# Linear attention and a tanh-shrink MLP on one core: reading the state one product ahead of the output, issuing eight half loads from GpSimd, and making the last unit's inner factors after another product

## The chip, the core and the metric

The kernel runs on one core of a Trainium2 chip. The core has a matrix engine (PE, with its weight loads shown as PEld), a vector engine (DVE), an activation engine (ACT), GpSimd (POOL) and a queue engine (SP). Each takes its instructions in the order of its own queue and waits on semaphores for what the others have made. Transfers are issued here from SP and POOL, a few from ACT at the very start, and all are carried by the same 16 DMA engines.

The metric is the device time of one execution in microseconds (us). The kernel before takes 670.73 us, the median of three runs between 670.1 and 672.22. An execution that was profiled gives the times inside.

## The reference

Chunks of decayed linear attention run along the sequence with one state per batch and head; then each token goes through a two-layer network with `h - tanh(h)` between the layers.

```python
# q, k, v: (B=4, H=8, S=768, D=64); lam: one decay per head
for b in range(nb):                                   # blocks of 64 positions
    intra = einsum('bhic,bhjc->bhij', qb, kb) * Dmask[None]
    intra = einsum('bhij,bhjd->bhid', intra, vb)
    inter = einsum('bhid,bhde->bhie', qb * lam_pow[None], kv_state)
    out[:, :, sl] = intra + inter
    kv_state = lam_block * kv_state + einsum('bhsd,bhse->bhde', kb * rev_pow, vb)

x = out.transpose(0, 2, 1, 3).reshape(3072, 512)
h = x @ w_in                                          # 512 x 2048
result = (h - tanh(h)) @ w_out                        # 2048 x 512
```

The two weight matrices come as 64-bit floats; the kernel makes 32-bit floats of them itself.

## The kernel before

**Tiling.** The kernel takes 128 positions of all four batches at a time, so there are six groups g of 512 tokens. Within a group a chunk (g, b) is one batch's 128 positions. The attention of a group is done for two pairs of batches, (0, 1) and (2, 3). The hidden layer's 2048 columns are four units u of 512. Block products are done by Strassen-like schemes with seven products (P1 to P7) in place of eight: from group 1 on for the output layer (`down`, `down_twice`), where most of the seven are themselves made of seven smaller ones, and for groups 2 to 5 for the input layer too (`inner_steps`).

**Attention of a chunk pair.** `att_transpose` turns q and k round (on PE for groups 0 and 1, on DVE later) and makes `qd`, the decayed q. `att_scores` makes the masked scores `ss`. `att_out` then issues, on PE: products that read the old state into two PSUM banks `ops` (line 420, 32 small ones in a pair); on ACT, four decays of the state in place (line 423), which may only begin when those reads are done; on PE, products with the scores (line 429), the new key-value products (line 394), and more score products (line 439), which carry an explicit dependency on the first of the four decays; on DVE the sum of state and key-value products (line 449); on ACT the two evacuations to `xt` (line 451).

**The first 104 us.** Group 0's input layer is done plainly by `up_plain(u, cs)` (line 798): for one unit and one quarter c of its output, 16 matmul records of 256 columns in the trace, then a tanh on ACT (line 805) and a subtraction on DVE (line 806). While these products run, the raw weights are loaded, rounded on ACT (lines 309 to 311, three operations a block) and DVE (lines 313 and 314, two operations a block), and four staging tiles `raw64` go round: a load waits until ACT has read the block four before it. Blocks of `w_in` are loaded from SP (lines 226 and 229), blocks of `w_out` from POOL (line 224). A list `turns` says which quarter product comes next, how many blocks to round after it, and which piece of group 1's attention to run: `p0` for batches 0 and 1, `p1` for 2 and 3. `p0[2:]`, the decays of k and `att_out(1, (0, 1))`, stands behind the product (3, 21).

**Loads of q, k and v.** `load_natural` brings a chunk in one transfer for q and three each for k and v: heads 0 to 3 in one, and heads 4 to 7 in two, with the two halves of 64 rows exchanged. For group 0 the exchanged halves come from ACT (batch 0) or POOL; from group 1 on all come from SP. Chunks (1, 0) and (1, 1) are asked for by `load(B + 2)`, on line 891, ahead of the `turns`; the blocks of `w_in` that are not yet asked for stand behind them in SP's queue.

**Group 1 on.** The hidden layer of a group runs over units u. At the end of each unit of group 1, `inner_weights(u)` makes the inner factors of that unit's `w_in`, which group 2 on will use: for each of three factors, four small additions on DVE (line 572) into a tile of the ring `sums` (six tiles, shared with the sums that `sums_twice` and `inner_tokens` make) and one store of 192 KB from POOL to DRAM (line 573). Group 1's output products follow in this order: P2, `att_out(2, (0, 1))`, P4, the transposes of batches 2 and 3, P5, their scores, the decays of k (line 385), P6, `att_out(2, (2, 3))`, P7, then P3 together with group 2's inner products. Within `down_twice` the seven small products come in the order 1, 2, 6, 5, 7, 3, 4; the sixth needs a sum that DVE makes while the product runs (line 748). The factors of the small products come from DRAM through a ring of seven tiles `wb`, issued by POOL (lines 648, 651 and 654), each load waiting until PE has left the tile seven before it.

**What sets the order.** The framework's planner lays out each engine's queue, taking operations that it holds for ready, the earlier in the program first. Operations wrapped in `tied` or `keep_in_program_order` keep the order of the program among each other: all loads of q, k and v, the DVE transposes (line 349), the additions of `inner_weights` and the decays of k of group 2 are of this kind. Everything else may be drawn ahead.

Of the kernel before, what the change touches and what calls it, by code (L numbers as in the profile page):

```python
# [9 lines left out]
F32 = mybir.dt.float32  # L10
# [14 lines left out]
def kernel(  # L25
# [32 lines left out]
    nc = tc.nc  # L58
# [75 lines left out]
    chunks = [(g, b) for g in range(NG) for b in range(B)]  # L134
    at = {"loaded": 0}

    def load_natural(g, b, names):
        for name, src, bufs in (("q", q, 2), ("k", k, 3), ("v", v, 4)):
            if name in names:
                x = (qpool if name == "q" else io).tile([128, H, D], F32, name=f"{name}_nat", tag=name, bufs=bufs)  # L140
                rows = src[b, :, ts(g, BLK), :].rearrange("h s d -> s h d")
                if name == "q":
                    parts = [(nc.sync, x, rows)]
                else:
                    eng = nc.sync if g > 0 else nc.scalar if b == 0 else nc.gpsimd
                    parts = [(nc.sync, x[:, 0:4], rows[:, 0:4])] + [
                        (eng, x[ts(1 - t, HALF), 4:8], rows[ts(t, HALF), 4:8]) for t in range(2)]
                for eng, to, of in parts:
                    tc.keep_in_program_order(eng.dma_start(out=to, in_=of))
                raw[g, b][name] = x  # L150

    hold = {}

    def load_blocks(g, half):

        for name, src in (("q", q), ("k", k)):
            x = late["blk"].tile([128, 2 * NP, BLK // 32, 32], F32, name=f"{name}_blk", tag="blk")
            heads = src[ts(half, 2)].rearrange("b (p j) s d -> j s (b p) d", j=2)
            for r in range(BLK // 32):
                for c in range(4):  # L160
                    op = tc.keep_in_program_order(nc.sync.dma_start(
                        out=x[ts(c, 32), :, r], in_=heads[c // 2, g * BLK + 32 * r:g * BLK + 32 * (r + 1), :, ts(c % 2, 32)]))
                    if g in hold:

                        tc.add_manual_dep(op.ins, hold.pop(g).ins.name, mybir.DependencyInfo(
                            mybir.DependencyClass.Sync, mybir.DependencyReason.DATA), reason="begin")
            for n in range(2):
                raw[g, 2 * half + n][name + "b"] = x[:, ts(n, NP)]

# [230 lines left out]
        kv = kv_products(g, bs)  # L400
        tied(True, nc.scalar.activation(state[:, bs[0]:bs[0] + 2], kv, AF.Copy))

    def att_out(g, bs):
        half = bs[0] // 2
        xt[g, half] = xpool.tile([128, KI, HB], F32, name=f"xt{half}", tag=f"xt{half}")
        st = state[:, bs[0]:bs[0] + 2]

        ops = [bank("op", "att", 4).rearrange("d (p b s) -> d p b s", p=2, b=2) for _ in range(2)]

        def dst(n, p, j):  # L410
            return ops[p // 2][ts(j if p < 2 else 1 - j, 64), p % 2, n, :]

        decayed = None
        if g > 0:
            for n, b in enumerate(bs):
                for p in (0, 1):
                    for j in range(2):
                        r = ts(j, 64)
                        for pp in (p, p + 2):
                            nc.tensor.matmul(out=dst(n, pp, j), lhsT=state[r, b, pp, :], rhs=tr[g, b][2][r, pp, :],  # L420
                                             start=n == 0 and p == 0, stop=False, skip_group_check=True)
            for p in (3, 2, 1, 0):
                op = nc.scalar.activation(st[:, :, p, :], st[:, :, p, :], AF.Copy, scale=fwd[:, p, BLK - 1:BLK])
                decayed = decayed or op
        for n, b in enumerate(bs):
            ss, vn = sc[g, b], raw[g, b]["v"]
            for p in range(NP):
                for j in range(2):
                    tied(g == 0, nc.tensor.matmul(out=dst(n, p, j)[:, HALF:BLK], lhsT=vn[:, 2 * p + j, :],
                                                  rhs=ss[:, j, 2 + p, :], start=g == 0 and n == 0 and p % 2 == 0,  # L430
                                                  stop=n == 1 and p % 2 == 1, skip_group_check=True))
        kv = kv_products(g, bs) if 0 < g < NG - 1 else None
        for n, b in enumerate(bs):
            ss, vn = sc.pop((g, b)), raw[g, b]["v"]
            for x in range(2):
                for j in range(2):
                    for p in (x, 2 + x):
                        r = ts(p // 2, HALF)
                        op = nc.tensor.matmul(out=dst(n, p, j)[:, 0:HALF], lhsT=vn[r, 2 * p + j, :],
                                              rhs=ss[r, j, x, :], start=False, stop=n == 1 and x == 1,  # L440
                                              skip_group_check=True)
                        tied(g == 0, op)
                        if decayed is not None:


                            tc.add_manual_dep(op.ins, decayed.ins.name, mybir.DependencyInfo(
                                mybir.DependencyClass.Sync, mybir.DependencyReason.DATA), reason="rows")
# [322 lines left out]
    def every(steps):  # L770
        for _ in steps:
            pass
# [15 lines left out]
    def up_plain(u, cs):  # L788

        hm = {}  # L790
        for c in cs:
            a, t = divmod(c - 11, 10)
            hm[c] = bank("h", ("ya", "yb", "z", "w")[2 * t + a], 1).rearrange("q (m c) -> q m c", m=2)
        for i in range(KI):
            for c in cs:
                a, t = divmod(c - 11, 10)
                for m in range(2):
                    tied(u == 0, nc.tensor.matmul(  # L798
                        out=hm[c][:, m, :], lhsT=w1[u][:, i, a, ts(m, 128)], rhs=xt[0, t][:, i, :],
                        start=m == 0 and i == 0, stop=i == KI - 1, skip_group_check=True))  # L800
                if (i, c) != (KI - 1, cs[-1]):
                    yield
        for c in cs:
            th = work.tile([128, 2, HB], F32, name="th", tag="th")
            nc.scalar.activation(th, hm[c], AF.Tanh)
            nc.vector.tensor_tensor(hidden(0, c)[:, u], hm[c], th, op=AL.subtract)
        yield

# [85 lines left out]
             (3, 22, 1, ())]  # L894
    for u, c, n, more in turns:
        every(up_plain(u, (c,)))
        weights(ready["done"] + n)
        run(more)
        if c == 22:
            sums_first(u)  # L900
            if u == 1:
                load_weights(NU * KI)
                load(2 * B)
                powers()
            if u == 2:
                sums_in(0)
# [23 lines left out]
    for g in range(1, NG):  # L930
# [3 lines left out]
        for u in range(NU):  # L934
            if g < GI:
                for n in (2, 6, 5, 7, 1, 4, 3):
                    if n != 1:
                        up(g, u, n)
                    elif u + 1 < NU:
                        up(g, u + 1, 1)  # L940
                    else:
                        every(p_first)
                    if g == 1 and u < 2 and n == 5:
                        sums_in(u + 2)
            else:
# [12 lines left out]
                if not last and u < 2:  # L958
                    att_transpose(g + 1, (u,))
                elif not last:  # L960
                    if u == 2:
                        att_scores(g + 1, (0,))
                    att_decays(g + 1, (u - 2,))
            if g == GI - 1:
                inner_weights(u)
            if not last and u > 1 and g < GI:
                run(p0[u - 2:u - 1])
# [11 lines left out]
        sums_twice(g, 6)  # L979
        every(down_twice(g, 5, "w"))  # L980
        run(p1[1:2])
        if not last:
            att_decays(g + 1, (2, 3))
        if twice(g, 7):
# [58 lines left out]
```

## Time and profile before

| what | value |
|---|---|
| time, median of 3 runs (lowest, highest) | 670.73 us (670.1, 672.22) |
| time of the profiled execution | 669.47 us |
| its span, first to last instruction | 667.7 us |
| DVE busy | 470.7 us, 70% of the span |
| ACT busy | 244.9 us, 37% |
| POOL busy | 216.6 us, 32% |
| PE busy in 0 to 104 us | 93.07 us |
| PE busy in 104 to 155 us | 49.46 us of 51 |
| PE busy in 155 to 218 us | 63.00 us of 63 |
| PE busy in 218 to 257 us | 36.74 us of 39 |
| PE busy in 282 to 386 us, a full later group | 103.92 us of 104 |
| granted PE clock, mean over the span | 0.992 |

A busy PE is one with a matmul somewhere in its pipeline, so the table shows where it stood still, not how well it was used. The granted clock is the share of full speed that PE was allowed. An engine can also stand with work queued, behind an instruction whose semaphore has not come; the views of waits say which engine's event ended such a pause.

### The profile page before, as it was taken

What the parts mean: (1) busy time and instruction counts of PE and PEld (TensorE: products, weight loads), DVE (VectorE), ACT (ScalarE), POOL (GpSimd) and SP (SyncE); (2) the same over time, 40 slices, a digit from 0 to 9 for tenths busy, and PEclk for the clock granted to TensorE, in tenths of its full rate; (3) what the DMA queues carried; (4) which work ended last, traced back from release to release, by engine and by line L of the source; (5) the groups of instructions that cost most, each with busy time, mean ns of one, the idle gap of its engine ahead of it and who ended that gap; (6) DMA issues with size and microseconds to landing.
All of it is one profiled execution on the core that took longest, in us unless ns stands there. A gap on an engine that the chain in (4) does not pass through costs nothing.

```text
span 667.7 us, 14973 instructions
## 1 busy us (share of the span) xinstructions
PE 649.5 (97%) x5856; PEld 592.0 (89%) x5856; DVE 470.7 (70%) x888; ACT 244.9 (37%) x485; POOL 216.6 (32%) x374
## 2 busy tenths in 40 slices
PE   6899899999999989999999999999999999999998
PEld 6788688888888889988999988899988899998897
DVE  4476887975777985668986568986468887366843
ACT  2895954522331213442213543213353123263110
POOL 2200353894122535300354400254400145410151
PEclk8999999999999999999999999999999999999999
DMA  9989983999553866965487965486965377721295
GB/s 203 223 171 234 271 298 111 304 294 281 106 112 108 249 214 217 238 126 102 142 277 214 235 141 106 127 263 216 246 149 108 91 245 213 225 91 33 81 301 170
DMA packets 156662, 125.79 MB, mean 188 GB/s; under 512 B 128368, under 2 KB 129520, under 8 KB 156592
## 3 DMA queue, kind: packets, MB, share of 16 engines
q0 software_dynamic: 28864, 94.13, 45.6%
q1 hardware_dynamic: 126496, 30.43, 23.2%
q8 instruction: 46, 0.75, 0.5%
q10 hardware_dynamic: 1232, 0.27, 0.3%
q14 instruction: 24, 0.20, 0.1%
HBM read 103.81 MB, written 20.97 MB: 187 GB/s over the span
## 4 chain that ended last, share of the span: by engine, by line
PE 79%; DVE 6%; DMA 5%; issue 5%; ACT 4%; POOL 1%; SPq 0%; DVEq 0%; POOLq 0%; ACTq 0%
PE y L517 17%; PE y L743 12%; PE zw L743 9%; PE z L517 6%; PE y L601 6%; PE y L689 5%; PE w L689 4%; PE h L798 4%; PE acc L827 3%; PE z L601 3%; DMA raw<-in_moe_w_out_dram 3%; PE sp L374 1%; PE kv L394 1%; PE w L601 1%; PE end L782 1%
## 5 line engine op out<-in xcount | busy, mean ns | idle before, releaser
L651 POOL DMA_DIRECT2D wb<-fine x168 | 90.6, 540 | 205.3 <-PE y L689 72.5
L746 ACT ACTIVATE q<-y 128x128 f32<-128x128 f32 x96 | 26.6, 277 | 150.6 <-PE y L743 149.7
L798 PE MATMUL h<-xt,w 128*128 128x256 f32 x256 | 59.8, 391 | 2.5 <-DVE w L314 2.5
L743 PE MATMUL y<-wb,g 128*128 128x128 f32 x456 | 60.6, 278 | 0.0
L798 PEld LDWEIGHTS h<-xt,w 128*128 128x128 f32 x256 | 48.8, 194 | 10.7 <-DVE w L314 2.6
L743 PEld LDWEIGHTS y<-wb,g 128*128 128x128 f32 x456 | 55.1, 192 | 0.9
L654 POOL DMA_DIRECT2D wb<-factors x44 | 23.8, 542 | 87.0 <-PE y L689 49.0
L525 ACT ACTIVATE th<-g 128x512 f32<-128x512 f32 x40 | 25.2, 630 | 70.3 <-DVE g L543 53.6
L517 PE MATMUL y<-xt,w 128*128 128x256 f32 x192 | 45.0, 379 | 0.0
L526 DVE TENSOR_TENSOR g<-g,th 128x512 f32<-128x512 f32 x40 | 27.6, 691 | 21.0 <-ACT th L525 21.0
L517 PEld LDWEIGHTS y<-xt,w 128*128 128x128 f32 x192 | 36.4, 190 | 5.1 <-ACT g L534 0.2
L743 PE MATMUL zw<-wb,g 128*128 128x128 f32 x304 | 40.3, 275 | 0.0
L517 PE MATMUL y<-tt,ws 128*128 128x256 f32 x160 | 38.5, 379 | 0.0
L517 PE MATMUL y<-tt,w 128*128 128x256 f32 x160 | 38.1, 381 | 0.0
L517 PE MATMUL z<-xt,ws 128*128 128x256 f32 x160 | 38.1, 381 | 0.0
L689 PE MATMUL y<-wb,g 128*128 128x256 f32 x160 | 37.3, 379 | 0.0
L743 PEld LDWEIGHTS zw<-wb,g 128*128 128x128 f32 x304 | 37.0, 192 | 0.2 <-DVE g L748 0.2
L689 PE MATMUL w<-wb,g 128*128 128x256 f32 x160 | 35.5, 380 | 0.0
L827 PE MATMUL acc<-wt,g 128*128 128x256 f32 x144 | 33.2, 381 | 1.5 <-DVE g L834 0.8
L689 PEld LDWEIGHTS y<-wb,g 128*128 128x128 f32 x160 | 30.4, 190 | 4.1
L689 PEld LDWEIGHTS w<-wb,g 128*128 128x128 f32 x160 | 30.3, 190 | 4.2
L517 PEld LDWEIGHTS y<-tt,w 128*128 128x128 f32 x160 | 30.2, 190 | 4.2
(195 smaller groups left out, 1458.7 us busy)
## 6 DMA issues: line engine op xcount, KB each, us to landing
wb<-fine POOLq DMA_DIRECT2D x168, 256.0 KB, 3.7
wb<-factors POOLq DMA_DIRECT2D x44, 256.0 KB, 4.7
wb<-fine_in POOLq DMA_DIRECT2D x36, 256.0 KB, 3.9
raw<-in_moe_w_out_dram POOLq DMA_DIRECT2D x16, 512.0 KB, 5.7
raw<-in_moe_w_in_dram SPq DMA_DIRECT2D x8, 512.0 KB, 6.2
raw<-in_moe_w_in_dram SPq DMA_DIRECT2D x16, 256.0 KB, 5.7
fine<-f POOLq DMA_DIRECT2D x16, 256.0 KB, 4.3
q_blk<-in_q_dram SPq DMA_DIRECT2D x128, 32.0 KB, 3.4
```

The lines of the kernel that those rows point to most:

```text
L374: tied(g == 0, nc.tensor.matmul(out=sp[j][ts(r, HALF), x:3 + p:2 + p - x, :], lhsT=k0, rhs=qj.rearrange("d (t i) -> d t i", t=2), start=Tr ...
L517: nc.tensor.matmul(out=t[:, m, :], lhsT=wt[:, kt, ts(m, 128)], rhs=x[:, kt, :], start=first and m == 0 and kt == 0, stop=kt == 1, skip_gro ...
L525: nc.scalar.activation(th, src, AF.Tanh)
L526: nc.vector.tensor_tensor(dst(c), src, th, op=AL.subtract)
L601: nc.tensor.matmul(out=dst[:, ts(u, 128)], lhsT=a, rhs=b, start=x in (1, 2, 5) and u == 0, stop=True, skip_group_check=True)
L651: nc.gpsimd.dma_start(out=t.rearrange("p m c -> p (m c)"), in_=fine[TWICE.index(n_), SUB.index(x_)].rearrange("p u c -> p (u c)"))
L654: nc.gpsimd.dma_start(out=t, in_=factors[XAT[FACT[n_][1]]][:, 2 * x_:2 * x_ + 2, :])
L689: nc.tensor.matmul(out=t[:, m, :], lhsT=a[:, u, kt, ts(m, 128)], rhs=wb[:, kt, :], start=first and u == 0 and m == 0 and kt == 0, stop=u = ...
L743: nc.tensor.matmul(out=dst, lhsT=a[:, u, :], rhs=wb[:, ts(u, 128)], start=x in (1, 2) and u == 0, stop=u == NU - 1, skip_group_check=True)
L746: nc.scalar.activation(keep, dst, AF.Copy)
L798: tied(u == 0, nc.tensor.matmul(out=hm[c][:, m, :], lhsT=w1[u][:, i, a, ts(m, 128)], rhs=xt[0, t][:, i, :], start=m == 0 and i == 0, stop= ...
L827: nc.tensor.matmul(out=acc[n][:, r, :], lhsT=a[:, ts(r, 128)], rhs=b, start=kt == 0 and r == 0, stop=kt == KH - 1, skip_group_check=True)
```

## The change

Three parts, in three places.

**Loads.** The exchanged halves of k and v for chunks (1, 0) and (1, 1), eight transfers of 64 KB, are issued by POOL and no longer by SP. The first of them gets a dependency on the tanh of the quarter product (0, 11). Later chunks stay on SP.

**State read.** `att_out` is split: the new `att_read` takes the two PSUM banks, issues the 32 products that read the state, and the four decays of the state. For group 1's batches (0, 1) it is called right after the product (3, 11), while the rest of `att_out` stays behind (3, 21). All other calls of `att_out` call `att_read` at their own beginning, as before.

**Inner factors.** `inner_weights(3)`, for the last unit, moves from the end of group 1's unit loop to behind P5 and the scores of batches 2 and 3, ahead of the decays of k.

```diff
-                    eng = nc.sync if g > 0 else nc.scalar if b == 0 else nc.gpsimd
+                    eng = nc.sync if g > 1 or (g, b) >= (1, 2) else nc.scalar if (g, b) == (0, 0) else nc.gpsimd
...
-                    tc.keep_in_program_order(eng.dma_start(out=to, in_=of))
+                    op = tc.keep_in_program_order(eng.dma_start(out=to, in_=of))
+                    if eng is nc.gpsimd and g in hold:
+                        wait_for(op, hold.pop(g))
...
+    def att_read(g, bs):
         ops = [bank("op", "att", 4).rearrange("d (p b s) -> d p b s", p=2, b=2) for _ in range(2)]
         decayed = None
         if g > 0:
+            st = state[:, bs[0]:bs[0] + 2]
...
+                            nc.tensor.matmul(out=out_dst(ops, n, pp, j), lhsT=state[r, b, pp, :],
+                                             rhs=tr[g, b][2][r, pp, :], start=n == 0 and p == 0, stop=False,
+                                             skip_group_check=True)
             for p in (3, 2, 1, 0):
                 op = nc.scalar.activation(st[:, :, p, :], st[:, :, p, :], AF.Copy, scale=fwd[:, p, BLK - 1:BLK])
                 decayed = decayed or op
+        reads[g, bs] = ops, decayed
...
+        if (g, bs) not in reads:
+            att_read(g, bs)
+        ops, decayed = reads.pop((g, bs))
...
-            nc.scalar.activation(th, hm[c], AF.Tanh)
+            op = nc.scalar.activation(th, hm[c], AF.Tanh)
+            if (u, c) == (0, 11):
+                hold[1] = op
...
         every(up_plain(u, (c,)))
+        if (u, c) == (3, 11):
+            att_read(1, (0, 1))
...
-            if g == GI - 1:
+            if g == GI - 1 and u + 1 < NU:
                 inner_weights(u)
...
         run(p1[1:2])
+        if g == GI - 1:
+            inner_weights(NU - 1)
         if not last:
             att_decays(g + 1, (2, 3))
```

`wait_for(op, other)` is the explicit dependency that the kernel before writes out at two places.

More of the change, by code (lines that the diff above doesn't have):

```diff
@@ L135, with wait_for @@
     at = {"loaded": 0}
+    hold = {}
+    def wait_for(op, other):
+        tc.add_manual_dep(op.ins, other.ins.name, mybir.DependencyInfo(
+            mybir.DependencyClass.Sync, mybir.DependencyReason.DATA), reason="begin")
     def load_natural(g, b, names):
@@ L148, in load_natural @@
                 for eng, to, of in parts:
-                    tc.keep_in_program_order(eng.dma_start(out=to, in_=of))
+                    op = tc.keep_in_program_order(eng.dma_start(out=to, in_=of))
+                    if eng is nc.gpsimd and g in hold:
+                        wait_for(op, hold.pop(g))
                 raw[g, b][name] = x
-    hold = {}
     def load_blocks(g, half):
@@ L163, in load_blocks @@
                     if g in hold:
-                        tc.add_manual_dep(op.ins, hold.pop(g).ins.name, mybir.DependencyInfo(
-                            mybir.DependencyClass.Sync, mybir.DependencyReason.DATA), reason="begin")
+                        wait_for(op, hold.pop(g))
             for n in range(2):
@@ L401, in att_state, with out_dst @@
         tied(True, nc.scalar.activation(state[:, bs[0]:bs[0] + 2], kv, AF.Copy))
[L403 to L406, printed above, removed]
+    reads = {}
+    def out_dst(ops, n, p, j):
+        return ops[p // 2][ts(j if p < 2 else 1 - j, 64), p % 2, n, :]
+    def att_read(g, bs):
         ops = [bank("op", "att", 4).rearrange("d (p b s) -> d p b s", p=2, b=2) for _ in range(2)]
-        def dst(n, p, j):
-            return ops[p // 2][ts(j if p < 2 else 1 - j, 64), p % 2, n, :]
         decayed = None
         if g > 0:
+            st = state[:, bs[0]:bs[0] + 2]
             for n, b in enumerate(bs):
@@ L419, in att_out @@
                         for pp in (p, p + 2):
-                            nc.tensor.matmul(out=dst(n, pp, j), lhsT=state[r, b, pp, :], rhs=tr[g, b][2][r, pp, :],
-                                             start=n == 0 and p == 0, stop=False, skip_group_check=True)
+                            nc.tensor.matmul(out=out_dst(ops, n, pp, j), lhsT=state[r, b, pp, :],
+                                             rhs=tr[g, b][2][r, pp, :], start=n == 0 and p == 0, stop=False,
+                                             skip_group_check=True)
             for p in (3, 2, 1, 0):
@@ L424, in att_out, with dst @@
                 decayed = decayed or op
+        reads[g, bs] = ops, decayed
+    def att_out(g, bs):
+        half = bs[0] // 2
+        xt[g, half] = xpool.tile([128, KI, HB], F32, name=f"xt{half}", tag=f"xt{half}")
+        st = state[:, bs[0]:bs[0] + 2]
+        if (g, bs) not in reads:
+            att_read(g, bs)
+        ops, decayed = reads.pop((g, bs))
+        def dst(n, p, j):
+            return out_dst(ops, n, p, j)
         for n, b in enumerate(bs):
@@ L443, in att_out @@
                         if decayed is not None:
-                            tc.add_manual_dep(op.ins, decayed.ins.name, mybir.DependencyInfo(
-                                mybir.DependencyClass.Sync, mybir.DependencyReason.DATA), reason="rows")
+                            wait_for(op, decayed)
         if kv is not None:
```

## The prediction

> **What bounds the kernel now.** I read the page's engine shares first, then PE's waits, then the stretches around each wait, and last the queues that feed the engines named there. PE is the engine to watch:
>
> ```profile
> PE 649.5 (97%) x5856; PEld 592.0 (89%) x5856; DVE 470.7 (70%) x888; ACT 244.9 (37%) x485; POOL 216.6 (32%) x374
> ```
>
> From 155 to 218 us and from 257 us on PE hardly stops, so what it gains before 257 us should stay to the end. PE's own waits, the lines that bear on this change:
>
> ```profile
> PE h L798 <- DVE w L314: 2.5, 4, 1.1
> PE op L439 <- ACT state L423: 1.9, 1, 1.9
> PE zw L743 <- DVE gS L748: 1.7, 1, 1.7
> PE kv L394 <- DVE k_nat L385: 0.5, 1, 0.5
> ```
>
> (total us, times, longest). By the timeline, three of the four L798 waits lie at 61.55, 69.53 and 72.07 us (0.21, 0.24 and 0.98 us), the fourth (1.11) at 21.64, before anything changed; L439 waits at 79.3 to 81.1; L394 and L743 at 222.2 and 236.4. The stretches after the L439 wait:
>
> ```profile
> 79.20:81.10 1.90, 0.07 (x4) 0.00 (x0) 1.76 (x4) 1.90 (x6) 0.83 (x2) 1.00 0.81 294
> 82.00:83.00 1.00, 1.00 (x4) 0.80 (x4) 0.97 (x4) 1.00 (x3) 0.58 (x1) 0.59 0.74 83
> 83.00:84.00 1.00, 1.00 (x4) 0.82 (x3) 1.00 (x3) 1.00 (x2) 0.74 (x2) 0.50 0.75 211
> ...
> 85.00:86.00 1.00, 1.00 (x5) 0.86 (x4) 1.00 (x2) 1.00 (x3) 1.00 (x2) 0.71 1.14 387
> ```
>
> (stretch, its length, busy PE, PEld, DVE, ACT and POOL, then the granted clock.) Right behind the wait PE ran at half clock: 0.41, 0.50, 0.50 and 0.29 us of full speed are lost from 82 to 86. What is late at the source is ACT and, ahead of it, SP:
>
> ```profile
> 40.92 2.82 SPq L149 DMA_DIRECT2D k_nat<-in_k_dram  x3
> 43.84 3.09 SPq L149 DMA_DIRECT2D v_nat<-in_v_dram  x3
> 52.38 1.21 SPq L229 DMA_DIRECT2D raw<-in_moe_w_in_dram  x2
> 58.36 0.67 ACT L309 ACTIVATE w<-raw 128x512 f32<-128x512 f32 x1 [2.00 <-DMA raw<-in_moe_w_in_dram]
> 80.39 1.26 ACT L423 ACTIVATE state<-state,fwd 128x128 f32<-128x128 f32 x4
> ```
>
> SP is taken by loads of chunks (1, 0) and (1, 1) from 40.23 to 52.3 us; the weight blocks behind them come late, ACT does nothing but four tanhs from 47.5 to 58.4, is then full (10.00 and 9.26 us of the next two tens), and runs the decays 3.1 us after the state was read (L420 ended at 77.25).
>
> **Loads.** The eight halves leave SP: 0.68, 1.54, 0.62, 1.11, 0.60, 0.61, 0.60 and 0.61 us by their rows, about 6.4 us. The six loads left pass, and the next block of weights is issued at about 46.0 instead of 52.38. Its staging tile was read by ACT at 40.8, so nothing else holds it. By its landing time (4.7 us median for its two transfers) ACT starts at about 52 instead of 58.36, and its full stretch moves by 6 us. On POOL eight issues at 0.62 us (the rows of group 0's halves) cost 5.0 us, where POOL does nothing between 20 and 62.4. The new wait ends with the tanh at about 36.5, so they go out from 36.6 to 41.6 and land by 48.7 (4.1 to 7.1 us in those rows); the transposes want them at 62.5. Behind the waiting instruction stand only the other seven and the first `w_out` load, at 62.43 before. The bytes compete with three `w_in` blocks: 0.5 MB at 186 to 244 GB/s (stretches 40 to 42 and 36 to 38) is 2.1 to 2.8 us; the third of those blocks was rounded at 48.5 and is wanted by PE at about 53.8, so 5.3 us cover it. Without that cover it would be up to 2.8 us lost. **Gain:** the three waits on L314, 0.21 + 0.24 + 0.98 = 1.4 us; bounds 0 and 1.6 (with the 0.20 us wait on ACT's evacuation at 65.48).
>
> **State read.** 32 products of 1.03 us and four decays of 1.26 us are moved, none added. The read is released 3.5 us earlier (one quarter product, 16 records from 91.76 to 95.3), so even with ACT's old backlog the first decay ends at about 80.8 - 3.5 = 77.3 while L439 is ready at 79.27. Two PSUM banks are held 3.5 us longer. Of the four the scores use, DVE frees two by 69.94 and the others by 71.4; the read now comes at about 70.2, so the bound of a new wait is 0 to 1.2 us. I take 0, since two banks suffice. **Gain:** 1.9 us, and the half clock behind it. The 32 product records from 81.75 ended at 90.02, 8.27 us; at the pace of the next 32 (16 in 3.5 us) they take 7.0. I take 1.3; bounds 0 and 1.7, the lost shares above.
>
> A page weighed against this row: the Trainium skill, TensorE: Matmul & The Clock Gate, section "Why this matters for your kernels", asks only that PE have no idle gaps of more than about 3 us. By it a pause of 1.86 us would not lower the clock, the dip would have another cause, and the 1.3 would not be gained. The trace speaks for the link here (the dip starts 1.3 us after the pause), and against it at 236 us, where 1.69 us of pause are followed by a clock of 1.00.
>
> **Inner factors.** DVE works all but without a stop from 211.7 to 239, and this is the chain that ends there:
>
> ```profile
> 214.53 0.20 DVE ws L572
> 217.88 0.60 DVE ws L572 x3
> 231.31 0.34 DVE q L753
> 235.72 0.61 DVE gS L748
> 236.37 1.16 PE zw L743 x8
> ```
>
> Twelve additions at 0.20 us in the chain leave it: 2.4 us. L394's wait (0.47) goes, and a gap of 0.2 at 228.1 with it. P5's sixth product is then wanted at about 233.7. DVE cannot be 2.4 us earlier: L753 waits for P4's last products, now at 229.5, and from L753 to the end of L748 are 4.9 us with nothing free between (four transposes, two multiplications), giving 234.2 to 234.4. PE waits 0.5 to 0.7 instead of 1.69. Gain 0.47 + 0.2 + 1.1 = 1.7; bounds 0 and 2.4. The work is paid later: 2.4 us of DVE between P5's last transposes and the decays of k. Ahead of P6's L748, wanted at about 241.9, DVE had 0.3 us idle at 239. The ring `sums` matters more: P5 frees two tiles, and the third factor wants the first one's tile back, that is its store issued (0.76 us) and landed (3.2 us median, 6.3 at most). 234.9 + 0.8 + 3.2 is 238.9, then 0.9 for the additions, 1.2 for two decays and 0.7 for L748: 241.7, just in time. With 6.3 it is 3 us late. On POOL three stores, 2.3 us, slip between loads of the `wb` ring, which has 0.36 us free in each 0.89; before, POOL had 2.3 us free at 235.5 to 237.8. I charge 0.5 us for P6 and POOL together; bounds 0 and 3.
>
> **Sum.** 1.4 + 1.9 + 1.3 + 1.7 - 0.5 = 5.8 us. The profiled execution took 669.47 (span 667.7, 1.8 around it), 1.26 below the median of 670.73. So 663.7 for such an execution and **664.9** for the median.
>
> **The rivals.**
> *Absorbed.* From 52.3 to 110.4 the chain of waits holds almost no PE: it goes from the raw loads over POOL, ACT and DVE to the first output products, where PE waits 0.83 us at 110.42. DVE is busy 9.07 and 9.15 us of the two tens from 80 to 100. If DVE and the stores of `fine` stay where they are, PE arrives 4.6 us early at 110 and waits there; only the inner factors' 1.7 are left: 669.0. Against it: the chain begins with the loads that come 6 us earlier, and DVE stood idle for 5.5 us between 50.2 and 56.4.
> *The clock dip stays*, by the page's rule: 664.9 + 1.3 = 666.2.
> *The third tile.* If one of the two tiles that P5 frees goes to another sum, `inner_weights` needs two round trips to DRAM, each 0.2 + 0.76 + 3.2 to 6.3. From 234.9 DVE is released between 243 and 249.5, P6's L748 ends 2.8 us after that, and PE, wanting it at 241.9, stands for 4 to 10 us, 7 in the middle, with 1.3 for the clock behind so long a pause, in place of the 0.5 charged: 664.9 - 0.5 + 8.3 = 672.7. It decides from 5.0 us of standing (664.4 + 5.0 + 1.3 = 670.7). For it: six tiles, of which P6 and P7 hold four. Against it: the factors come earlier in the program than what competes.
> *Not as it says.* The planner may put the decays on ACT behind the same roundings, and the loads may not come earlier because of a staging tile. Then only odd tenths move: 670.5.
>
> **How the numbers follow.** Forecast 0.57, absorbed 0.14, dip stays 0.11, third tile 0.13, not as it says 0.05. The forecast's own range is 662 to 668; the low end is all bounds gained, 1.6 + 1.9 + 1.7 + 2.4 = 7.6, and the 0.83 at 110 us with them. Up to 671 for the others, so about 0.17 is left out. 0.3% or 2.0 us is what a measurement tells from no change: faster is below 668.7, the forecast, the dip case and 0.4 of absorbed, 0.74; slower is above 672.7, some 0.7 of the third tile (standing is spread unevenly to its long side), 0.09; the rest is 0.17.
>
> **What would show it.** Raw `w_in` issues at 46, ACT's rounding from 52, POOL's eight issues at 36.6; no PE wait on L423, clock 1.00 throughout 75 to 100; first output products at about 99.5, with PE's wait there no larger than 0.8 (larger: absorbed). In group 1, no wait at L394, P5's wait at 0.5, and P6 without a wait on L748 (with one, the third tile). A half clock again behind a shorter pause would make the 1.3 wrong.

## The result, and the profile after

| | median of 20 runs | lowest, highest | profiled execution | its span |
|---|---|---|---|---|
| before | 669.96 us | 668.31, 672.22 | 669.47 us | 667.7 us |
| after | 673.94 us | 670.73, 677.44 | 675.61 us | 673.8 us |

After takes 1.0061 of before's time, with a 95% interval from 1.0043 to 1.0078: **slower by about 4.1 us**, where 5.8 us of gain were forecast. The profiled execution of after is 1.67 us above its median, so its 6.1 us of longer span overstate the loss.

PE is still the engine to watch. The row of engine shares on after's page:

```profile
PE 650.8 (97%) x5856; PEld 592.7 (88%) x5856; DVE 469.6 (70%) x888; ACT 244.8 (36%) x485; POOL 221.3 (33%) x382
```

The waits of PE in after that answer to those of before, and the new ones (total us, times, longest; code lines are 3 to 18 higher than before's, so L814 is before's L798, L456 is L439, L427 is L423, L759 is L743):

```profile
PE h L814 <- DVE w L319: 5.0, 4, 2.0
PE zw L759 <- DMA wb<-fine: 2.1, 2, 1.7
PE op L456 <- ACT state L427: 2.1, 1, 2.1
...
PE acc L845 <- DVE g L851: 1.5, 1, 1.5
...
PE op L423 <- DVE ss L385: 1.1, 1, 1.1
PE end L798 <- DMA wb<-factors: 1.1, 1, 1.1
PE zw L759 <- DVE g L764: 1.0, 1, 1.0
```

The two waits that were to go stand here undiminished: on the rounded weights 5.0 us in place of 2.5 (3.0 of them behind 60 us, where before has 1.4), on the decays 2.1 in place of 1.9. The waits at L394 (0.5) and on `gS` in P5 (1.7) did go. PE ran at half clock again behind the wait on the decays, which ended at 83.73 (stretch, length, busy PE, PEld, DVE, ACT, POOL, then the granted clock):

```profile
84.00:85.00 1.00, 1.00 (x33) 0.82 (x23) 1.00 (x4) 1.00 (x3) 0.34 (x1) 0.88 1.05 153
85.00:86.00 1.00, 1.00 (x4) 0.81 (x3) 1.00 (x4) 1.00 (x2) 1.00 (x2) 0.50 0.64 230
86.00:87.00 1.00, 1.00 (x4) 0.81 (x3) 0.89 (x3) 1.00 (x3) 0.08 (x1) 0.50 0.94 319
```

At the source, SP's timeline in after (start, length, engine, line, transfers and their number):

```profile
42.27 0.58 SPq L155 DMA_DIRECT2D q_nat<-in_q_dram  x1
42.96 0.52 SPq L155 DMA_DIRECT2D k_nat<-in_k_dram  x1
43.58 0.45 SPq L155 DMA_DIRECT2D v_nat<-in_v_dram  x1
44.12 5.25 SPq L155 DMA_DIRECT2D q_nat<-in_q_dram  x1
...
52.50 1.19 SPq L234 DMA_DIRECT2D raw<-in_moe_w_in_dram  x2
```

Six loads pass in place of fourteen, and yet the next block of weights is issued at 52.50 (before: 52.38). Part of this is a later start: the first of the loads goes out at 42.27 (before: 40.23), and this start also differs between kernels whose loads are all on SP (39.63 in e6, 41.29 in e2). Counted from it, the next block is issued after 10.23 us in place of 12.15, so SP saves 1.9 us where 6.4 were forecast. SP stands for 5.25 us in a single load, q of chunk (1, 1), while POOL's eight transfers, issued from 38.94 to 43.8, are under way. ACT shows what else moved. Its timeline in after:

```profile
58.46 0.67 ACT L314 ACTIVATE w<-raw 128x512 f32<-128x512 f32 x1 [5.37 <-DMA raw<-in_moe_w_in_dram]
59.04 0.58 ACT L821 ACTIVATE th<-h 128x512 f32<-128x512 f32 x1
...
81.31 0.58 ACT L821 ACTIVATE th<-h 128x512 f32<-128x512 f32 x1
81.77 0.78 ACT L315 ACTIVATE r<-raw 128x512 int16<-128x512 uint32 x1
82.40 1.27 ACT L427 ACTIVATE state<-state,fwd 128x128 f32<-128x128 f32 x4
```

In before, a tanh ran at 55.76, while the block of weights was still on its way; in after the tanh at 59.04 stands behind the waiting rounding. And the read of the state began at 74.43, 1.7 us earlier than before's 76.15, but the decays ran at 82.40, 2.0 us later, because roundings and a tanh stood ahead of them in ACT's queue.

To see where the 6.1 us lie, the span is cut at five events of PE's timeline: the first transposes of batches (0, 1) of group 1, the end of their L439 (L456 after), the first output product, the first up product of group 1, and the first of group 2's inner products in P3. Lengths in us between them, one execution each, with some of the kernels of the experiments:

| kernel | to L439's end | to the first output product | to group 1's up | to the inner products | to the end |
|---|---|---|---|---|---|
| before | 19.3 | 22.3 | 50.5 | 102.6 | 410.5 |
| after | 21.8 | 24.4 | 50.2 | 101.0 | 413.8 |
| loads alone (e1) | 26.2 | 22.4 | 50.0 | 102.6 | 411.3 |
| read alone (e2) | 18.0 | 21.3 | 53.2 | 102.6 | 411.0 |
| inner factors alone (e3) | 20.3 | 20.6 | 53.4 | 101.0 | 410.5 |
| loads on POOL, before's order (e5) | 18.2 | 20.6 | 52.6 | 102.6 | 412.2 |
| half loads left out, before's order (e8) | 18.8 | 20.6 | 53.3 | 102.6 | 410.7 |
| before, more tiles (e9) | 19.0 | 20.6 | 50.1 | 104.5 | 410.3 |
| read, more tiles (e11) | 17.1 | 22.1 | 50.0 | 102.6 | 410.9 |
| inner factors, more tiles (e12) | 20.2 | 20.6 | 49.5 | 100.8 | 410.5 |

After loses 4.6 us up to the first output product and 3.3 us behind group 2's first inner product, and wins 1.6 in group 1's output layer. The 22.3 of before and the 24.4 of after each hold 1.7 us lost at half clock behind the wait on the decays, and the 104.5 of e9 holds 1.7 us lost in the same way behind a pause at 234.9.

### The profile page after: what moved, and what is told of

It is laid out like the page before. It is cut to its first block, busy times and chain, and to the rows that moved or that the text cites. A ratio compares the mean times of both kernels' runs of the same rounds, so it can differ in the third digit from the quotient of the medians.

```text
span 673.8 us, 14979 instructions
## 1 busy us (share of the span) xinstructions
PE 650.8 (97%) x5856; PEld 592.7 (88%) x5856; DVE 469.6 (70%) x888; ACT 244.8 (36%) x485; POOL 221.3 (33%) x382
## 4 chain that ended last, share of the span: by engine, by line
PE 65%; issue 13%; DMA 8%; DVE 6%; ACT 4%; POOL 2%; SPq 1%; POOLq 0%; DVEq 0%; ACTq 0%
PE y L533 13%; PE y L759 10%; PE zw L759 7%; PE z L533 5%; PE y L617 5%; PE w L705 4%; PE y L705 4%; PE acc L845 4%; PE z L617 3%; DMA raw<-in_moe_w_in_dram 2%; DMA raw<-in_moe_w_out_dram 2%; PE sp L379 1%; PE op L423 1%; PE end L798 1%; DMA q_nat<-in_q_dram 1%
## 5 line engine op out<-in xcount | busy, mean ns | idle before, releaser
L814 PE MATMUL h<-xt,w 128*128 128x256 f32 x256 | 60.1, 391 | 5.0 <-DVE w L319 5.0
L759 PE MATMUL y<-wb,g 128*128 128x128 f32 x456 | 60.7, 278 | 0.0
L814 PEld LDWEIGHTS h<-xt,w 128*128 128x128 f32 x256 | 48.7, 194 | 13.4 <-DVE w L319 5.4
L759 PEld LDWEIGHTS y<-wb,g 128*128 128x128 f32 x456 | 55.1, 192 | 0.9
L759 PE MATMUL zw<-wb,g 128*128 128x128 f32 x304 | 40.3, 276 | 1.5 <-DVE g L764 1.0
L759 PEld LDWEIGHTS zw<-wb,g 128*128 128x128 f32 x304 | 37.0, 192 | 1.8 <-DVE g L764 1.2
```

Of the source, the lines that this page charges most:

```text
L759: nc.tensor.matmul(out=dst, lhsT=a[:, u, :], rhs=wb[:, ts(u, 128)], start=x in (1, 2) and u == 0, stop=u == NU - 1, skip_group_check=True)
L814: tied(u == 0, nc.tensor.matmul(out=hm[c][:, m, :], lhsT=w1[u][:, i, a, ts(m, 128)], rhs=xt[0, t][:, i, :], start=m == 0 and i == 0, stop= ...
```

## The experiments

Each kernel was timed beside before on the same chip; ratios are to before there.

### One part at a time

e1 makes only the first part of the change (POOL issues the eight halves, behind the tanh of (0, 11)), e2 only the second (`att_read`), e3 only the third (`inner_weights(3)` behind P5), e4 the second and third. The line of each part (e1, e2, e3) that sets it going:

```diff
-                    eng = nc.sync if g > 0 else nc.scalar if b == 0 else nc.gpsimd
+                    eng = nc.sync if g > 1 or (g, b) >= (1, 2) else nc.scalar if (g, b) == (0, 0) else nc.gpsimd
...
+        if (u, c) == (3, 11):
+            att_read(1, (0, 1))
...
-            if g == GI - 1:
+            if g == GI - 1 and u + 1 < NU:
                 inner_weights(u)
...
+        if g == GI - 1:
+            inner_weights(NU - 1)
```

> Only the eight half loads move from SP to POOL (with the dependency on the tanh); the state read and the inner factors stay as before. Theory A (the loads part is the loss: SP is held by what its queue can take, not by issuing, so the weight blocks are asked for no earlier, while the planner, which believes in earlier blocks, has drawn ACT's roundings ahead of tanhs and decays): slower than before by 4 to 7 us, 674 to 677, with ACT standing 4 us or more at a rounding for a raw block between 50 and 60 us and the first block after the loads issued by SP at 52 to 53 us. Theory B (the loads part is what I predicted, the loss is elsewhere): faster by 1 to 2 us, 668 to 669, SP issuing that block at about 46 us.

> Only the state read and its decays move ahead of the product (3, 21). Theory A (sound by itself, spoilt by the loads part, which puts the decays on ACT behind roundings and a tanh): no PE wait on the decays, clock 1.00 behind it, faster by 2 to 3 us, about 667. Theory B (the read itself costs: PE's queue stands at it for banks or decayed q): a PE wait of 1 us or more at the read, same or slower, 670 to 672.

> Only the last unit's inner factors move behind P5. Theory A (as predicted): PE's waits of 0.47 us at the key-value products and 1.69 us in P5 go, a wait of up to 1.1 us in P6 comes; faster by 1 to 2 us, about 668.5. Theory B (the third tile of the ring, or the late loads of wb that the changed kernel's profile shows in the last group, belong to this part): P6 waits 2 us or more, or waits on wb of 1 to 3 us past 600 us; same or slower, 670 to 673.

> The changed kernel with the loads part undone. Theory A (the loads part alone turns the change into a loss): faster than before by 3.5 to 5 us, about 665.5, near the sum of the two parts alone. Theory B (the loss lies in one of these two parts or in their meeting): 670 or more.

| kernel | median | before | ratio, 95% interval |
|---|---|---|---|
| e1, loads alone | 676.31 | 670.88 | 1.0082 [1.0062, 1.0103] |
| e2, read alone | 670.2 | 670.88 | 0.9993 [0.998, 1.0006] |
| e3, inner factors alone | 669.2 | 670.88 | 0.9977 [0.9961, 0.9993] |
| e4, read and inner factors | 668.85 | 670.88 | 0.9966 [0.9948, 0.9984] |

The whole loss, and more, comes with the loads part: alone it costs 5.5 us. Without it the change is 2.3 us faster than before, less than the 3.5 to 5 expected of e4. e2 meets neither of its theories: the wait on the decays goes, and the time hardly moves. ACT's timeline in e1 shows the decays even later than in after:

```profile
80.21 0.59 ACT L821 ACTIVATE th<-h 128x512 f32<-128x512 f32 x1
...
84.34 0.59 ACT L821 ACTIVATE th<-h 128x512 f32<-128x512 f32 x1
84.81 0.79 ACT L316 ACTIVATE r<-raw 128x512 f16<-128x512 f32 x1
85.43 1.27 ACT L427 ACTIVATE state<-state,fwd 128x128 f32<-128x128 f32 x4
```

PE waited 6.72 us for them. Before had the decays at 80.39, although its blocks of weights came no earlier.

### Transfers or order

The loads part does two things: it moves eight transfers, and it makes the planner lay out all queues anew. These can be parted. e5 has e1's loads, with the instructions of PE, DVE, ACT and POOL held to before's order; e6 has before's loads in e1's order. e7 is the whole change in e4's order. The order is held by dependencies that cost no semaphore:

```diff
+        for names in planned:
+            names = [f"I-{n}" for n in names if f"I-{n}" in byname]
+            for x, y in zip(names, names[1:]):
+                if byname[x].engine == byname[y].engine:
+                    tc.add_manual_dep(byname[y], x, mybir.DependencyInfo(
+                        mybir.DependencyClass.NoSync, mybir.DependencyReason.DATA), reason="order")
```

e8 is e5 without the eight transfers. The exchanged halves of k and v of chunks (1, 0) and (1, 1) are set to zero by POOL, so those heads are left out of its attention.

```diff
-                    op = tc.keep_in_program_order(eng.dma_start(out=to, in_=of))
+                    if eng is nc.gpsimd and g == 1:
+                        op = tc.keep_in_program_order(nc.gpsimd.memset(to, 0.0))
+                    else:
+                        op = tc.keep_in_program_order(eng.dma_start(out=to, in_=of))
```

> The eight half loads come from POOL as in the loads part alone, but PE, DVE, ACT and POOL keep the instruction order that the planner had made for the kernel before (pinned by order-only dependencies). Theory A (the loss is the planner's new order, made for weight blocks that it takes to land earlier): the 5.5 us of loss go, 669 to 671.5 beside a before of about 670.5; SP still held to 51 us or later by the load of q. Theory B (the loss is the transfers' own: eight more from POOL crowd the DMA engines and the weight blocks land later): 674 or more.

> The loads stay on SP as before, but PE, DVE, ACT and POOL get the order that the planner had made with the loads part. Theory A (the order is the loss): 674 to 677, ACT standing 4 us or more at a rounding between 50 and 60 us and PE waiting 4 us or more on the decays. Theory B (the transfers are the loss): 669 to 671.5.

> The whole change, with PE, DVE, ACT and POOL in the order that the planner made for the state read and the inner factors alone. Theory A: near the kernel with those two parts alone (668.85), 667.5 to 670. Theory B (the loads on POOL cost by themselves): 672 or more.

> As the loads from POOL in the old order, but the eight halves are not loaded at all: GpSimd writes zeros in their place, so that part of k and v of two chunks of group 1 is left out. Theory A1 (SP stands in the second load of q because POOL's transfers share the DMA engines with it): that load is issued in under 2 us instead of about 5, and the next weight block is asked for at 46 to 48 us. Theory A2 (SP's own queue is full of small packets whatever POOL does): it still takes 3 us or more, the weight block at 50 us or later.

| kernel | median | before | ratio, 95% interval |
|---|---|---|---|
| e5, new loads, old order | 671.93 | 670.75 | 1.0014 [0.9996, 1.0032] |
| e6, old loads, new order | 676.35 | 670.75 | 1.0095 [1.0067, 1.0122] |
| e7, whole change, old order | 669.5 | 670.75 | 0.9978 [0.9962, 0.9994] |
| e8, no half loads, old order | 670.38 | 670.75 | 0.9988 [0.9967, 1.001] |

**It is the order.** Old transfers in the new order lose 6.4 us, as much as e1 within the intervals; new transfers in the old order lose 0.9, and by the interval at most 2.1. The whole change, held to the other order, turns from a loss of 0.6% into a gain of 0.2%. ACT's timeline in e6 shows why:

```profile
57.51 0.66 ACT L314 ACTIVATE w<-raw 128x512 f32<-128x512 f32 x1 [9.21 <-DMA raw<-in_moe_w_in_dram]
58.08 0.58 ACT L821 ACTIVATE th<-h 128x512 f32<-128x512 f32 x1
```

ACT stood 9.21 us at a rounding whose block had not landed, with tanhs behind it; in before two of them ran in that time, at 52.31 and 55.76. Why the planner put it there was not tested. A reading that fits the two orders is that, with the halves gone from SP's queue, it holds the blocks of `w_in` for early and so draws the roundings ahead of tanhs and decays.

**The blocks were little earlier, and that alone gains nothing.** The load of q of chunk (1, 1) and the next block in SP's timeline, in e5:

```profile
43.50 5.17 SPq L155 DMA_DIRECT2D q_nat<-in_q_dram  x1
...
51.38 1.94 SPq L234 DMA_DIRECT2D raw<-in_moe_w_in_dram  x2
```

and in e8, where POOL moves nothing:

```profile
42.98 2.77 SPq L158 DMA_DIRECT2D q_nat<-in_q_dram  x1
...
48.60 1.19 SPq L237 DMA_DIRECT2D raw<-in_moe_w_in_dram  x2
```

So of SP's stand of 5.17 us, 2.4 go with POOL's transfers running beside it and 2.8 remain without them; this lies between what the two theories expected, and neither holds alone. Even with a block issued 3.8 us earlier than before's 52.38, e8 is not measurably faster than before. ACT's timeline in e8 shows one reason:

```profile
55.91 0.60 ACT L824 ACTIVATE th<-h 128x512 f32<-128x512 f32 x1 [2.86 <-PE h L817]
56.40 0.67 ACT L317 ACTIVATE w<-raw 128x512 f32<-128x512 f32 x1
```

The rounding at 56.40 waits for no transfer. In before's order it stands behind a tanh that needs a product of PE, and so starts 2.0 us earlier than before's 58.36, not the 6 forecast. PE's three waits on the rounded weights that the loads were to remove are still there, 0.21, 0.24 and 0.81 us (before: 0.21, 0.24, 0.98). An order between e1's and before's was not tried.

### What takes the read's gain back

In e2 the wait on the decays is gone and the clock stays at 1.00, yet the time does not fall. PE comes to the output products 2.3 us sooner than in before, counted from the first transposes, and the stretch behind grows by 2.7. But e5 and e8, which have before's order and the read where it was, ran at full clock behind their wait and come to the output products in 38.9 and 39.4 us, where e2 takes 39.3: in these executions, one of each kernel, the 2.3 us are largely before's half clock and not the wait. DVE's timeline in e2 and, below it, PE's:

```profile
104.52 0.69 DVE L300 TENSOR_TENSOR f<-wt,f 128x512 f32<-128x512 f32 x1 [2.89 <-DMA fine<-f]
...
106.93 0.68 DVE L465 TENSOR_TENSOR state<-state,kv 128x512 f32<-128x512 f32 x1
```

```profile
107.67 2.07 PE L843 MATMUL acc<-wt,g 128*128 128x256 f32 x8 [1.06 <-DVE state L465]
110.84 2.83 PE L843 MATMUL acc<-wt,g 128*128 128x256 f32 x12 [1.10 <-DVE g L850]
```

DVE stands 2.89 us at a sum `f`, for whose tile the store of an earlier one to DRAM must have landed. Behind it in DVE's queue are `g` and the sum of the state, and PE stands for those. The same sum in before and, below it, in e8:

```profile
104.09 0.69 DVE L295 TENSOR_TENSOR f<-wt,f 128x512 f32<-128x512 f32 x1 [2.20 <-DMA fine<-f]
```

```profile
104.07 0.69 DVE L303 TENSOR_TENSOR f<-wt,f 128x512 f32<-128x512 f32 x1 [4.23 <-DMA fine<-f]
```

It begins at nearly the same time although PE comes to the output products at 104.14 in before, 102.89 in e2 and 102.09 in e8. To test whether this stand takes the gain back, two of the four tiles get room of their own:

```diff
-                 (1, 5, [io.tile([128, 4, 128], F32, name="f4", tag="v", bufs=4) for _ in range(4)])]
+                 (1, 5, [io.tile([128, 4, 128], F32, name="f4", tag="v", bufs=4) for _ in range(2)] + [
+                     stage.tile([128, 4, 128], F32, name="f4", tag="f4", bufs=2) for _ in range(2)])]
```

The orders of PE, ACT and SP stay as they were; DVE's and POOL's move by a few sums and stores. e9 is before with these tiles, e10 is e4, e11 is e2 and e12 is e3 with them.

> Kernel before, with one change: two of the four f4 tiles of sums_fine (the sums f that VectorE makes and that are stored to fine) come from a tag of their own in the pool stage instead of the ring v that they share with k_nat, v_nat and the rest; four more tiles' room in all. The orders of PE, ACT and SP are unchanged. In before, the wait of f on the store of fine (line 295) is 2.2 us at about 104, but PE arrives at the first output products only at 104.1 and stands there about 2.7 us in all. Theory 'the stand of VectorE at the store of fine takes back what an earlier arrival gains': the wait on the store shrinks below 0.5 us, the stretch from the first output products to group 1's up products falls from 50.5 to 49.5 to 50.3, time 0 to 1 us below before, ratio 0.9985 to 1.0. Rival 'the floor of that stretch is set later (raw w_out blocks and the roundings behind them)': the wait shrinks just so, the stretch stays at 50.5, ratio 0.999 to 1.001.

> e4_read_and_inner (state read ahead and inner factors behind P5, loads as before) with the same two f4 tiles from a tag of their own. In e4 VectorE stood 2.9 us at line 300 on the store of fine at 104.5, and PE stood at the output products on state (1.06), on g of line 850 (1.10) and on g of line 849 (1.51); the stretch was 53.2 us against before's 50.5 though PE came 1.2 us earlier. Theory 'the stand at the store absorbs the read': the wait at line 300 falls below 0.5 us, PE's waits there on state and g of line 850 fall to 0.3 or less each, the stretch falls to 50.0 to 51.5, time 665.5 to 667.5, ratio 0.992 to 0.995, 2 to 3 us below e4. Rival 'floor set later': the wait at line 300 goes, PE's waits move to later output products (g, or the weights of w_out), the stretch stays at 52.5 to 53.5, ratio 0.996 to 0.998 as e4 had.

> The state read ahead alone (e2) with the two f4 tiles from a tag of their own (e9); the instructions of PE, ACT and SP in e2's order. With before, e2 and e9 it makes a square: read ahead or not, tiles or not. Theory 'the read saves its wait and the half clock behind it, and the stand of VectorE at the store took this back in e2': 1.2 to 3 us below e9 on the same chip (e9 was 0.9977 of before), ratio 0.993 to 0.996. Rival 'the read moves a wait that is paid again wherever PE is held next': ratio 0.9965 to 0.9985, no more than e9 had by the tiles alone, with new waits of PE on DVE between 80 and 102 (lines 385 and 823 of g and ss) that sum to over 1 us.

> The inner factors behind P5 alone (e3) with the two f4 tiles; e10 is this and the read ahead. Inner factors alone were 0.9977, tiles alone 0.9977, both with the read 0.9944. Theory 'the read saves something once the tiles are there': slower than e10, ratio 0.9955 to 0.9975. Rival 'the read is worth nothing, tiles and inner factors add up': ratio 0.994 to 0.9955, as e10, PE waits on the decays (ACT state) of 1.2 to 2.3 us still there at about 81.

| kernel | median | before | ratio, 95% interval | same without the tiles |
|---|---|---|---|---|
| e9, tiles alone | 669.23 | 671.59 | 0.9977 [0.9958, 0.9996] | 1 |
| e11, read | 668.66 | 670.84 | 0.9961 [0.9943, 0.9979] | 0.9993 (e2) |
| e12, inner factors | 668.57 | 670.84 | 0.995 [0.993, 0.997] | 0.9977 (e3) |
| e10, read and inner factors | 668.01 | 671.59 | 0.9944 [0.9923, 0.9964] | 0.9966 (e4) |

**The stand at the store costs time, with the read and without it.** In all four the wait on `fine` is gone there, the stretch behind the first output product is 49.5 to 50.1 us in place of the 53.2 to 53.4 of e2 to e4, and the tiles are worth 0.22 to 0.32% wherever they are added, for before too. But they are worth as much without the read (0.23 and 0.27%) as with it (0.32 and 0.22%), so nothing here shows that this stand was what kept the read's gain back. e9's gain of 1.5 us is beyond the 0 to 1 that the theory had given it, and its profiled execution, with a span of 667.6 us beside before's 667.7, does not show it. e10's gain over e4, 1.5 us by the ratios, is short of the 2 to 3 expected.

**The read stays small even so.** The pairs e9 and e11, e12 and e10 put it at 0.16% and 0.06%, 0.4 to 1.1 us, which these intervals cannot tell from nothing, nor, pair by pair, from the 1.9 us of the wait; e2 by itself gained 1.3 us at most by its interval. PE's timeline in e11:

```profile
80.25 0.69 PE L457 MATMUL op<-ss,v_nat 64*64 64x64 f32 x32
...
89.74 3.72 PE L815 MATMUL h<-xt,w 128*128 128x256 f32 x16 [0.38 <-DVE g L823]
...
98.89 1.56 PE L424 MATMUL op<-qd,state 64*64 64x128 f32 x32 [0.27 <-DVE ss L386]
```

and in e12, without the read:

```profile
82.44 0.69 PE L457 MATMUL op<-ss,v_nat 64*64 64x64 f32 x32 [2.15 <-ACT state L428]
83.06 6.74 PE L815 MATMUL h<-xt,w 128*128 128x256 f32 x30
...
100.09 1.10 PE L424 MATMUL op<-qd,state 64*64 64x128 f32 x32
```

e11 has no wait on the decays, but from there to the first output product it takes 22.1 us, and e12 takes 20.6. Of these 1.5 us, 0.65 are its smaller waits on DVE, less than the over 1 us that the rival wanted, and 0.46 are the 32 reads of batches (2, 3), which take 1.56 us in place of 1.10; why they do is not shown. This holds beyond the pair: the stretch is 21.3 to 22.3 us in the five kernels that have the read ahead and full clock there (e2, e4, e7, e10, e11), and 20.6 in each of the five without the read ahead and with full clock (e3, e5, e8, e9, e12). So 0.6 to 1.7 us of what the read saves are paid back before the first output product. e12 keeps the wait, at full clock behind it (30 products in 6.74 us, 8.43 in before). So e11's 0.9961 lies between the two theories, a gain of 1.1 us over e9's ratio where one asked for 1.2 and the other for none, and e12's ratio and wait are the rival's. e10 and e12 are the fastest kernels, faster than before and after; which of the two is faster is open.

## Why the prediction was wrong

**What bounds the kernel.** PE did. Of the idle times that the prediction set out to remove, two went when their part was made alone, the wait on the decays (e2) and those of the inner factors (e3). The waits on the rounded weights stayed, even with earlier blocks (e8).

**Loads.** The step that failed first: "The six loads left pass, and the next block of weights is issued at about 46.0 instead of 52.38." It came at 52.50, and counted from the first of the loads SP had saved 1.9 us of the 6.4. The prediction took the rows of the eight halves for time that each transfer costs SP by being issued. The transfers left took most of it back: 5.25 us in one that took 1.37 before. POOL's side was priced right (eight issues in 4.9 us, 5.0 forecast). The size of the competition, 2.1 to 2.8 us, fits too: counted from its first load, e8 has the next block 2.4 us earlier than e5. But it was charged to a block of `w_in` that had cover, and it fell on SP's queue. The next step failed as well, that "ACT starts at about 52 instead of 58.36": in e8, with the block issued at 48.60, it started at 56.40, behind a tanh. The gain of 1.4 us became nothing (e5: 1.0014). The Trainium skill, DMA: Bandwidth & Descriptors, section "Issuing engines are not separate DMA queues", says that transfers of all engines interleave on the same 16 DMA engines, so that a second issuer saves no more than the time of initiating them. The trace agrees in that only 1.9 of 12.15 us were saved; that this time is "usually small relative to the DMA itself" does not hold where SP stood for 5.25 us in one transfer.

**The order.** The larger failure was not a term of the sum at all. The working held every engine's queue as before's trace shows it and moved only the edited instructions. Yet the front of this document says that the planner lays out each queue from what it holds for ready, so moved loads move roundings, tanhs and decays as well. The rival *Not as it says* names just this, decays behind the same roundings, but with a chance of 0.05 and a time of 670.5, as if an order could only leave things as they are. It cost 5.5 us in e1 and 6.4 in e6.

**State read.** The release came 1.7 us earlier in after, and 3.5 were forecast; in e2, without the new order, the wait of 1.9 us went as foreseen, and no new wait for PSUM banks appeared. What failed is the sentence above it, "what it gains before 257 us should stay to the end": e2 gained about 0.5 us of the 3.2 forecast for the read and the half clock. Two terms were wrong. The move was charged with nothing ("moved, none added"), and 0.6 to 1.7 us of what it saves are paid back on the way to the first output product. And the 1.3 us of half clock were read from one execution: it came back in after, but behind the same wait PE ran at full clock in e3, e5, e8, e9 and e12. *Absorbed*, at 0.14, was right in part. Its condition, that the stores of `fine` stay where they are, held, and the wait at 110.42 in before was the trace of it; but with that stand gone the read is still worth only 0.4 to 1.1 us.

**Inner factors.** Right. Forecast 1.7 less 0.5; e3 gained 1.5 (0.9977), and its stretch from group 1's up products to group 2's inner products is 1.6 us shorter. P5's wait is gone altogether (0.5 forecast) and P6 has none on L748, so *The third tile* did not come. (The 6.3 us that it took for a store's longest landing belongs to a load of `wb<-fine_in`; the twelve stores of before landed in 2.5 to 3.6.) What is paid later fell on P7 instead, in PE's timeline of after:

```profile
257.26 1.16 PE L759 MATMUL zw<-wb,g 128*128 128x128 f32 x8 [1.04 <-DVE g L764]
```

**The sum.** Loads, and the order that came with them: 1.4 forecast, minus 5.5 measured. Read: 3.2 and 0.5. Inner factors: 1.2 and 1.5. Added up by the single parts that is 3.5 us slower, and after was 4.1 slower.

## What to carry to other kernels

Where a planner lays out the queues, an edit is a new order for every engine: compare the order of each engine's instructions before and after, and hold the old one by dependencies without semaphores to tell the order from the edit. Time in which an issuing engine stands in a transfer is not the price of that transfer; take it away and the next one may stand. Before an earlier arrival is booked as a gain, find the first wait behind it that does not move with it, here a sum that needs a tile back from a store. And a lowered clock that was seen in one execution is no price that a change is sure to earn back.

## What the runs showed that was not expected

**One load, many prices.** The load of q of chunk (1, 1), 256 KB in one transfer, held SP for 1.37 us in before, 0.55 in e6, 5.25 in after and 2.77 in e8; in the four kernels with the halves on POOL it is 4.94 to 5.62.

**Half clock behind a short pause comes and goes.** Behind pauses of 1.86 us (before) and 2.07 (after) at the same place PE ran some 3 us at a clock of 0.50; behind 2.27 (e3), 2.15 (e12), 2.03 (e8), 1.46 (e5) and 1.16 (e9) it stayed at 1.00. At 234.9 it fell to 0.50 behind 2.04 us in e9, and before's 1.69 at that place did not lower it. Behind 6.72 (e1), 6.64 (e6) and 3.64 (e6, at 60.72) the clock was 0.50 each time, and from 84 to 90 us in e1. The Trainium skill, TensorE: Matmul & The Clock Gate, section "Why this matters for your kernels", wants idle gaps of no more than about 3 us: the three long pauses fit it, and the three short ones with a lowered clock do not, so a pause below its bound isn't safe here.

**Late waits with the halves on POOL.** In the last group, 600 us after the eight transfers, PE waited for `wb<-factors` in each of the four kernels that have them, and in none of the other ten. In after's timeline of PE:

```profile
643.76 1.13 PE L759 MATMUL zw<-wb,gS 128*128 128x128 f32 x8 [1.67 <-DMA wb<-fine]
660.55 1.13 PE L759 MATMUL zw<-wb,g 128*128 128x128 f32 x8 [0.43 <-DMA wb<-fine]
663.65 7.26 PE L798 MATMUL end<-wb,g 128*128 128x256 f32 x48 [1.08 <-DMA wb<-factors]
```

e1, e5 and e7 have 0.37, 0.21 and 0.84 us at the last of these places. Waits on `wb<-fine` come late in others too (1.13 us in e10). The last column of the table of stretches is 411.3 to 413.8 us for these four (e5 412.2, e7 412.1) and 410.2 to 411.2 for the other kernels. These are single executions; the pairs e5 and before, e7 and e4 put it at about 0.1%, within their intervals. Why it should be so is open, and it wasn't tried.
